# Half of the column transforms by mirror, a third bank for the MLP and a second for the first value products: a fused attention, Fourier-mix and MLP kernel on one core

## The chip, the cores and the metric

The kernel runs on one core of one Trainium2 chip. The metric is the device time of one launch in microseconds (us); less is better. The kernel before takes 309.21 us, the median of three runs from 308.92 to 309.44.

## The reference, cut to what matters

The batch has 4 items of 768 rows. Each item goes through attention in chunks (8 heads of 64, rows attend to a window of their neighbours and to 8 memory rows), then through a Fourier mix over rows and columns, then through a normalized MLP:

```python
x = attention(q, k, v, mem_k, mem_v)         # 4 x 768 x 512
X = np.fft.fft(np.fft.fft(x, axis=1), axis=2)
u = x + np.real(X)
un = (u - mean(u)) / sqrt(var(u) + 1e-6)     # over the last axis
out = u + np.maximum(un @ w_ch1, 0) @ w_ch2  # 512 -> 2048 -> 512
```

`x` is real, so the real part of its transform is the same at (row k, column j) and at (row -k, column -j), counted round.

## The kernel before, in words

**Order of the work.** Every piece of work is a task with an engine, an estimated cost, the tasks that it comes after, and buffers that it takes and gives back. `Plan.order` (L62) runs these tasks through a small clock of its own and writes down the order in which they start. That order is fixed when the program is built: on the chip each engine takes its instructions strictly in it and waits on semaphores. So an estimate that is wrong costs a wait, and nothing behind the waiting instruction can pass it on that engine. MLP matmuls are marked as fillers: they go wherever nothing else can start.

**Attention** (L692, per batch item four pairs of heads). q and k come by POOL's DMA queue (L286) and v by SP's (L289). TensorE turns q and k (L309), forms scores (L344), ScalarE takes the exponential (L355), TensorE forms the products with the values (`e_values`, L363), and VectorE divides by the sum and writes the rows to `xsb` (`e_norm`, L376). Each pair is done in two halves g. The value products of all halves go through one PSUM bank, tag `xa`. In the first batch item, which has no MLP work beside it, `Plan.order` fills idle time of TensorE with dummy matmuls (`e_fill`, L651, the rows named `idle`) until the first Fourier rows can start.

**Fourier mix.** VectorE folds the rows by symmetry and splits them into two half-precision parts. `g_rows` (first item, L517) or `e_rows` (L433) transforms along the sequence into PSUM tiles `ps`. ScalarE and VectorE bring them to `up` (`e_up` L448, `e_rest` L454), and a reversed copy goes to `dn` (`e_dn`, L459). `e_columns` (L537) transforms along the columns for six row tiles kt: eight matmuls of 256 columns for each, from `up` for kt 0 to 2 and from `dn` for kt 3 to 5, into PSUM tiles `pm`. `e_sum` (L549) adds them to `xsb` and frees the bank. `e_stats` (L553) and `e_un` (L560) give the centred rows. They are turned for the MLP by TensorE in the first item, and by SP's DMA transposes in the others (`e_flip`, L572).

**MLP.** In two halves sh of 384 rows: sixteen tiles `ph` of four matmuls each (`e_ch1`, L593), each emptied by ScalarE (`e_relu`, L600), then three tiles `pc` of sixteen matmuls (`e_ch2`, L606), each emptied by VectorE (`e_osb`, L613) and stored from ScalarE's queue (`e_out`, L619).

**PSUM.** Of eight banks, `tr` and `xa` have one each, `sc` two, and the tags `acc` and `mlp` two each. `ps` and `pm` use `acc`; `ph` and `pc` use `mlp`, but in the last batch item every third of their tiles uses `acc` (`mtag`, L588).

Of the kernel before, what the change touches and what calls it, by code (L numbers as in the profile page):

```python
# [31 lines left out]
def strided(src, off, dims):  # L32
    return bass.AP(tensor=src.tensor, offset=src.offset + off,
                   ap=[list(src.ap[0])] + [list(d) for d in dims])
# [105 lines left out]
def kernel(  # L140
# [49 lines left out]
    seq = [(b, pr) for b in range(B) for pr in (0, 2, 1, 3)]  # L190

    plan = Plan(dict(qs=NS, ks=NS, va=NV, kTb=NKT, qT=2, tr=1, sc=1, xa=1, e1=3,
                     xsb=3, fold=2, hl=1, up=4, dn=4, acc=2, mlp=2, un=6, unT=2, hT=1, osb=3))
    add = plan.add
    MLPS = 1000000

# [165 lines left out]

    def e_values(n, g):  # L363
        e1 = e1_of.pop((n, g))
        xa = aps.tile([P, 3, 2, 66], FP32, tag="xa", bufs=1, name="xa")
        xa_of[n, g] = xa
        for st in range(3):
            for hh in range(2):
                v1 = va[n % NV]
                for half in range(2):  # L370
                    t6 = 2 * st + half
                    nc.tensor.matmul(xa[64 * half:64 * half + 64, st, hh, 0:65],  # L372
                                     e1[:, hh, t6, :], v1[:, hh, 6 * g + t6, 0:65],
                                     start=True, stop=True)
# [11 lines left out]
            xa[:, :, :, 0:D], zs.unsqueeze(3).to_broadcast([P, 3, 2, D]), ALU.mult)  # L386


    zy_of, pq_of, ff_of, hl_of, ps_of, up_of, pm_of, un_of, tp_of = ({} for _ in range(9))
    mu_of, unT_of, rstd_of, g_of = {}, {}, {}, {}  # L390
    mid = cpool.tile([P, 2, NST, 1], FP16)
    mid32 = cpool.tile([P, NST, 1], FP32)
    warm = cpool.tile([P, 1], FP32)
    gate = cpool.tile([P, 1], FP32)

    def e_zy(b, par, c):
# [60 lines left out]
                                up[:, 0].rearrange("p k s -> p s k"), ALU.subtract)  # L457

    def e_dn(b, par, ab):  # L459
        dn = fpool.tile([P, 2, HS], FP16, tag="dn", bufs=4, name="dn")  # L460
        nc.vector.tensor_copy(dn, rev_ap(up_of[b, par, ab][2], HS, HS, [[2 * NK, 2]]))
        up_of[b, par, ab][1] = dn

    def g_zy(par, g):
        if g == 0:
# [82 lines left out]

    def e_sum(b, kt):  # L549
        uv = xs[b][:, kt, :].rearrange("p (j c) -> p c j", c=2)  # L550
        nc.vector.tensor_tensor(uv, pm_of.pop((b, kt)), uv, ALU.add)  # L551

    def e_stats(b, kt):  # L553
        if kt == 0:
# [17 lines left out]
    def e_flip(b, kt):  # L572
        if kt == 0:
            unT_of[b] = fpool.tile([P, NDT, S], FP16, tag="unT", bufs=2, name="unT")
        nc.sync.dma_start_transpose(unT_of[b][:, :, ts(kt, P)], un_of.pop((b, kt)))

    def e_unT(b, kt):
        if kt == 0:
# [6 lines left out]
        nc.gpsimd.tensor_tensor(rstd, rstd, mhalf, ALU.pow)  # L585


    def mtag(b, i):  # L588
        return "acc" if b == B - 1 and i % 3 == 2 else "mlp"

    ph_of, pc_of, hT_of, osb_of = ({} for _ in range(4))

# [18 lines left out]
                             start=(ht == 0), stop=(ht == NHT - 1))  # L611

    def e_osb(b, sh, stl):  # L613
        st = sh * 3 + stl
        osb_of[b, st] = osb = fpool.tile([P, DM], FP32, tag="osb", bufs=3, name="osb")
        nc.vector.scalar_tensor_tensor(osb, pc_of.pop((b, sh, stl)), rstd_of[b][:, st:st + 1],  # L616
                                       xs[b][:, st, :], ALU.mult, ALU.add)

    def e_out(b, st):  # L619
        nc.scalar.dma_start(out[b, ts(st, P), :], osb_of.pop((b, st)))  # L620


    t_zero = add("DVE", 0.2, e_zero, rank=-21)
    t_table = add("ACT", 1.4, lambda: nc.scalar.activation(warm, zero, AFT.Sin), [t_zero], rank=-3)
# [67 lines left out]
    def attention(n):  # L692
        nonlocal t_gate
        b, pr = seq[n]
        first = b == 0
        lq, lk = [add("POOL", 0.9, lambda i=i: e_load_qk(n, i), take=(("qs", "ks")[i],),
                      moved=1.3 if b else (2.1, 2.1, 1.4, 1.4)[n], late=0.0 if b == 0 else 2.0,
                      behind=t_gate if n == HP else t_ck.get(n - 1),
                      rank={0: -4 + i, 1: -1.2 + 0.1 * i}.get(n)) for i in range(2)]
        lv = add("SP", 2.5, lambda: e_load_v(n), [t_ones[n] if n < NV else None],  # L700
                 take=("va",), moved=4.0 if b else (4.4, 6.5, 4.9, 3.6)[n], late=0.0 if b == 0 else 2.0)
        t_lv[n] = lv
        t_ck[n] = lk
        if n == HP - 1:
            def e_gate():
                nc.gpsimd.tensor_copy(gate[64:65], va[n % NV][64:65, 1, NT - 1, 0:1])

            t_gate = add("POOL", 0.1, e_gate, [lv])
        tq = add("PE", 0.40, lambda: e_turn_q(n), [lq, t_idb], take=("tr",), give=("qs",))
        dve = ("DVE", nc.vector.tensor_copy) if n < HP else ("ACT", None)  # L710
        eq = add("ACT", 0.80, lambda: e_qT(n), [tq], take=("qT",), give=("tr",),
                 rank=SINES - 0.5 if n == 0 else None)
        ktag = "acc" if first else "tr"
        tk = add("PE", 0.43, lambda: e_turn_k(n), [lk, t_idb, t_kz if n == 0 else t_kzs], take=(ktag,), give=("ks",))
        mk = t_mk[n] = add("DVE", 0.2, lambda: e_mkT(n), [t_mkT, t_kTz[n % NKT], t_mk.get(n - 1)],
                           take=("kTb",))
        ek = add(dve[0], 1.25 if dve[1] else 1.04, lambda: e_kT(n, dve[1]), [tk, mk], give=(ktag,))
        for g in range(2):
            s_ = add("PE", 0.32, lambda g=g: e_scores(n, g), [eq, ek], take=("sc",),
                     give=("qT", "kTb") if g == 1 else ())  # L720
            t_sc[n, g] = s_
            x_ = add("ACT", 2.4 if (n, g) == (0, 0) else 1.12, lambda g=g: e_exp(n, g),
                     [s_, t_masks, t_after.get(n)], take=("e1",), give=("sc",))
            tag = "xa"
            v_ = add("PE", 0.85, lambda g=g: e_values(n, g), [x_, lv, t_low[n % NV]], take=(tag,),
                     rank=len(plan.tasks) + (50 if (n, g) == (2, 1) else 25) if first else None,
                     give=("e1", "va") if g == 1 else ("e1",))
            take = ("xsb",) if g == 0 and n % HP == 0 else ()
            t_norm[n, g] = add("DVE", 0.78, lambda g=g: e_norm(n, g),
                               [v_, t_norm[n - n % HP, 0] if (n % HP, g) != (0, 0) else None],  # L730
                               take=take,
                               give=(tag,))
        return x_
# [60 lines left out]
    def first_fourier():  # L794
# [37 lines left out]
                                              give=(tag,))  # L832
        return columns_of(0, t_rest)

    def fourier(b):
        nrm = [[t_norm[b * HP + i, g] for i in ii for g in range(2)] for ii in ((0, 1), (2, 3))]
        t_rest = {}
        zy = {}
# [24 lines left out]
        return columns_of(b, t_rest)  # L863

    def columns_of(b, t_rest):
        t_dn = {}
        for par in range(2):
            for ab in range(2):
                t_dn[par, ab] = add("DVE", 0.36, lambda par=par, ab=ab: e_dn(b, par, ab),
                                    [t_rest[par, ab]], take=("dn",))  # L870
        t_un = {}
        allr = list(t_rest.values())
        cols = {}

        def columns(kt):
            cols[kt] = add("PE", 0.9, lambda: e_columns(b, kt),
                           allr + [t_rows] + (list(t_dn.values()) if kt > 2 else []),
                           take=("acc",), rank=len(plan.tasks) + (15 if kt == 3 else 0),
                           give=("up",) * 4 if kt == 2 else ("dn",) * 4 if kt == 5 else ())

        sa = None
        columns(0)
        for kt in range(NST):
            if kt + 1 < NST:
                columns(kt + 1)
            su = add("DVE", 0.7, lambda kt=kt: e_sum(b, kt), [cols[kt]], give=("acc",))
            sa = add("DVE", 0.9, lambda kt=kt: e_stats(b, kt), [su, sa])
            un = add("ACT", 0.72, lambda kt=kt: e_un(b, kt), [sa], take=("un",))
            if b > 0:
                t_un[kt] = add("SP", 0.1, lambda kt=kt: e_flip(b, kt), [un, t_un.get(kt - 1)],  # L890
                               take=("unT",) if kt == 0 else (), give=("un",), moved=0.8,
                               loose=True)
                continue
            tp = add("PE", 0.26, lambda kt=kt: e_turn_u(b, kt), [un, t_idh], take=("mlp",),
# [8 lines left out]
    def mlp(b, t_un, rs):  # L903
        for sh in range(2):
            relu = []
            c2 = None
            for ht in range(NHT):
                ph = add("PE", 0.65, lambda sh=sh, ht=ht: e_ch1(b, sh, ht),
                         mlp_prev + [t_un[3 * sh + i] for i in range(3)] + t_w1,
                         take=(mtag(b, ht),), give=("unT",) if sh == 1 and ht == NHT - 1 else (),  # L910
                         rank=MLPS + len(plan.tasks), filler=True)
                relu.append(add("ACT", 0.5, lambda sh=sh, ht=ht: e_relu(b, sh, ht),
# [1 line left out]
                                take=("hT",) if ht == 0 else (), give=(mtag(b, ht),),  # L914
                                rank=RELU(len(plan.tasks))))
            for stl in range(3):
                st = 3 * sh + stl
                for part in range(4):
                    end = part == 3
                    c2 = add("PE", 0.88, lambda sh=sh, stl=stl, part=part: e_ch2(b, sh, stl, part),  # L920
# [2 lines left out]
                             rank=MLPS + len(plan.tasks), filler=True)  # L923
                os_ = add("DVE", 0.76, lambda sh=sh, stl=stl: e_osb(b, sh, stl), [c2, rs],
                          take=("osb",), 
                          give=(mtag(b, stl), "xsb") if st == NST - 1 else (mtag(b, stl),),
                          rank=RELU(len(plan.tasks)))
                mlp_prev[0] = c2
                add("ACT", 0.1, lambda st=st: e_out(b, st), [os_], give=("osb",), moved=0.9,
                    rank=RELU(len(plan.tasks)))  # L930

# [46 lines left out]
```

## Time and profile before

| what | us |
|---|---|
| median of three runs | 309.21 |
| the profiled execution: its time | 308.85 |
| the profiled execution: its span | 307.1 |
| busy: TensorE matmuls / VectorE / ScalarE / GpSimd | 289.5 / 171.2 / 161.5 / 40.8 |
| first value products start on the chain | 20.97 |
| first Fourier rows start on the chain | 42.57 |
| last matmul ends | about 303.1 |

The span is what the profiler saw from the first instruction to the last event. A matmul row's mean time is that of one instruction from entry to end; several are in flight at once, so that the pieces in the chain, which lists work back to back, give the price of one more matmul better than the mean does. A row "a <- b" in the list of waits says that a stood idle until b had ended.

### The profile page before, as it was taken

To read this page: it belongs to the slowest core of one execution; us is meant where nothing else is said; L and a number is where in the kernel's file an instruction comes from. 1 tells how busy PE (TensorE), PEld (TensorE's weight loads), DVE (VectorE), ACT (ScalarE), POOL (GpSimd) and SP (SyncE) were. 2 spreads that over 40 slices of the span, in tenths; PEclk is the share of its full clock that TensorE was granted. 3 is DMA by queue.
4 is the path that set the end of the run, shared out by engine and by line. 5 is a ranking of instruction groups with operands and counts; after the bars stand their busy time and mean duration, and the time that the engine had idled before them with its cause. 6 is when DMAs were issued, how large, how long until landed. Compare 5 with 4: busy or idle time off the path is not lost.

```text
span 307.1 us, 7496 instructions
## 1 busy us (share of the span) xinstructions
PE 289.5 (94%) x3148; PEld 181.5 (59%) x3148; DVE 171.2 (56%) x371; ACT 161.5 (53%) x291; POOL 40.8 (13%) x78
## 2 busy tenths in 40 slices
PE   1399999999999999999989999999999999999994
PEld 1267678866666676666756646675554554554541
DVE  7877895975397887797764399476101001001001
ACT  6656373689884666885257423743360450531710
POOL 8806421132201102000020000000200000000000
PEclk9999999999999999999999999999999999999999
DMA  6989999999944925821361011004201101001011
GB/s 114 197 171 167 204 205 196 198 204 178 193 72 91 203 45 111 136 47 40 89 137 36 2 46 59 0 19 102 86 2 40 64 2 68 34 2 71 31 36 68
DMA packets 60289, 28.93 MB, mean 94 GB/s; under 512 B 48480, under 2 KB 56672, under 8 KB 60256
## 3 DMA queue, kind: packets, MB, share of 16 engines
q1 hardware_dynamic: 47168, 11.61, 21.0%
q0 software_dynamic: 9344, 10.49, 20.8%
q10 hardware_dynamic: 3744, 6.36, 5.7%
q8 instruction: 25, 0.41, 0.5%
q14 instruction: 8, 0.07, 0.1%
HBM read 30.28 MB, written 6.29 MB: 119 GB/s over the span
## 4 chain that ended last, share of the span: by engine, by line
PE 91%; DMA 2%; POOL 2%; DVE 1%; ACT 1%; issue 1%; POOLq 0%; ACTq 0%
PE ph L596 28%; PE pc L610 27%; PE xa L372 9%; PE pm L545 7%; PE ps L440 5%; PE idle L654 5%; PE ps L534 4%; PE sc L351 3%; DMA qs<-in_q_dram 2%; PE trk L313 2%; PE trq L313 2%; DVE osb L616 1%; POOL qs L286 0%; ACT hT L603 0%; PE tp L570 0%
## 5 line engine op out<-in xcount | busy, mean ns | idle before, releaser
L603 ACT ACTIVATE hT<-ph 128x384 f16<-128x384 f32 x128 | 60.9, 492 | 63.0 <-PE ph L596 51.5
L596 PE MATMUL ph<-unT,w_sb 128*128 128x384 f16 x512 | 91.6, 326 | 2.2 <-ACT hT L603 1.1
L610 PE MATMUL pc<-w_sb,hT 128*128 128x512 f16 x384 | 86.9, 379 | 0.0
L596 PEld LDWEIGHTS <-w_sb 128*128 128x128 f16 x512 | 47.8, 97 | 36.8 <-issue 5.7
L616 DVE SCALAR_TENSOR_TENSOR osb<-pc,rstd,xsb 128x512 f32<-128x512 f32 x24 | 18.0, 749 | 82.5 <-PE pc L610 82.4
L610 PEld LDWEIGHTS <-hT 128*128 128x128 f16 x384 | 36.8, 98 | 41.2 <-issue 0.2
L359 ACT ACTIVATE e<-sc,mbias 128x384 f32<-128x384 f32 x64 | 33.8, 583 | 13.8 <-PE sc L351 11.3
L372 PEld LDWEIGHTS xa<-va,e 128*64 128x64 f32 x768 | 25.0, 137 | 7.8 <-issue 7.0
L372 PE MATMUL xa<-va,e 128*64 128x65 f32 x768 | 29.3, 226 | 0.0
L563 ACT ACTIVATE un<-xsb,mu_s 128x512 f16<-128x512 f32 x24 | 17.2, 720 | 14.9 <-DVE mu_s L558 14.8
L382 DVE RECIPROCAL zs<-xa 128x6 f32<-128x6 f32 x32 | 6.1, 191 | 25.6 <-PE xa L372 25.5
L452 ACT CAST up<-ps 128x386 f16<-128x386 f32 x16 | 9.7, 603 | 19.1 <-PE ps L440 13.5
L551 DVE TENSOR_TENSOR xsb<-pm,xsb 128x512 f32<-128x512 f32 x24 | 16.0, 675 | 4.4 <-PE pm L545 4.2
L383 DVE TENSOR_TENSOR xsb<-xa,zs 128x384 f32<-128x384 f32 x32 | 17.8, 557 | 1.1
L557 DVE BATCH_NORM_STATS2 st<-xsb 128x6 f32<-128x512 f32 x24 | 16.4, 684 | 0.5
L654 PE MATMUL idle<-dz 128*128 128x384 bf16 x71 | 15.3, 350 | 1.0 <-DVE zero L230 1.0
L322 ACT COPY qT<-trq 128x768 bf16<-128x768 bf16 x16 | 12.8, 798 | 5.6 <-PE trq L313 5.5
L286 POOL DMA_DIRECT2D ks<-in_k_dram x16 | 10.2, 635 | 35.0 <-PE trk L313 31.4
L584 POOL TENSOR_SCALAR rstd<-mu_s 128x6 f32<-128x6 f32 x4 | 1.0, 245 | 102.0 <-DVE osb L616 57.7
L313 PE MATMUL trq<-ident_b,qs 96*64 96x96 bf16 x256 | 9.4, 221 | 5.1 <-DMA qs<-in_q_dram 5.1
L286 POOL DMA_DIRECT2D qs<-in_q_dram x16 | 10.5, 659 | 25.2 <-PE trq L313 21.5
L456 DVE TENSOR_TENSOR up<-ps,up 128x386 f16<-128x386 f32 x16 | 9.6, 598 | 7.5 <-ACT up L452 7.5
(126 smaller groups left out, 343.5 us busy)
## 6 DMA issues: line engine op xcount, KB each, us to landing
va<-in_v_dram SPq DMA_DIRECT2D x32, 220.0 KB
out_dram<-osb ACTq DMA_DIRECT2D x24, 256.0 KB
w_sb<-in_moe_w_ch_dram POOLq DMA_DIRECT2D x8, 512.0 KB, 16.9
qs<-in_q_dram POOLq DMA_DIRECT2D x16, 192.0 KB, 5.7
ks<-in_k_dram POOLq DMA_DIRECT2D x16, 192.0 KB, 6.1
va<-in_mem_v_dram SPq DMA_DIRECT2D x32, 24.0 KB
va<-in_v_dram SPq DMA_DIRECT2D x32, 22.0 KB
va<-in_v_dram SPq DMA_DIRECT2D x16, 32.0 KB
```

Source lines behind the costliest of these rows:

```text
L286: nc.gpsimd.dma_start(dst[n % NS][0:QP], src[b, 2 * pr:2 * pr + 2].rearrange("h (p j) d -> p h (j d)", j=RB))
L313: nc.tensor.transpose(out_[64 * hh:64 * hh + 64, j * w:(j + 1) * w], src[:, hh, j * D:(j + 1) * D], eye)
L359: nc.scalar.activation(e1[:, :, :, ts(half, 32)], sc[:, :, 0:6, ts(half, 32)], AFT.Exp, bias=mbias[:, half:half + 1], scale=1.0 / math.sqr ...
L372: nc.tensor.matmul(xa[64 * half:64 * half + 64, st, hh, 0:65], e1[:, hh, t6, :], v1[:, hh, 6 * g + t6, 0:65], start=True, stop=True)
L383: nc.vector.tensor_tensor(xs[b][:, 3 * g:3 * g + 3, 2 * pr * D:(2 * pr + 2) * D] .rearrange("p s (h d) -> p s h d", h=2), xa[:, :, :, 0:D] ...
L545: nc.tensor.matmul(pm[:, par, :], lhs, rhs[:, par, :], start=(im == 0), stop=(im == 3))
L563: nc.scalar.activation(un, xs[b][:, kt, :], AFT.Identity, bias=mu_of[b][:, kt, 0:1], scale=-1.0)
L596: nc.tensor.matmul(ph[:, 0:384], w1_sb[:, dt, ts(ht, P)], unT_of[b][:, dt, sh * 384:(sh + 1) * 384], start=(dt == 0), stop=(dt == NDT - 1))
L603: nc.scalar.activation(hT_of[b, sh][:, ht, :], ph_of.pop((b, sh, ht))[:, 0:384], AFT.Relu, bias=0.0, scale=-1.0)
L610: nc.tensor.matmul(pc_of[b, sh, stl], hT_of[b, sh][:, ht, ts(stl, P)], w2_sb[:, ht, :], start=(ht == 0), stop=(ht == NHT - 1))
L616: nc.vector.scalar_tensor_tensor(osb, pc_of.pop((b, sh, stl)), rstd_of[b][:, st:st + 1], xs[b][:, st, :], ALU.mult, ALU.add)
L654: nc.tensor.matmul(fill_of[0][:, 0:384], dz, strided(dz, 0, [[0, 3], [1, P]]), start=True, stop=True)
```

## The change

Four things are changed together.

1. For the second to fourth batch items only three column tiles are transformed. The other three are the same numbers read backwards. `e_sum_back` adds them, reversed, to a mirrored copy of the rows `xr`. `e_back` writes the last three row tiles of `xsb` to DRAM in reversed order, and `e_mirror` reads them back, both on POOL's queue. `e_last_row` transforms the one row that has no partner, into row 0 of the first `pm` tile. The `dn` copies of these items are gone. A `pm` bank is no longer freed by `e_sum` but by `e_sum_back`.
2. These mirrored row tiles reach the output backwards: `e_out_rows` stores them to DRAM in the order in which they lie, and `e_out_back` copies them from DRAM to DRAM on SP's queue, reversed by rows and with the columns set right. The MLP takes the row tiles of these items in the order 0, 3, 4, 5, 1, 2.
3. Every third MLP tile uses an `acc` bank in all batch items, not in the last alone.
4. In the first batch item every second value product (g = 1) goes to a bank of `mlp` (tile `xo`), so that two banks take turns.

```diff
     def e_values(n, g):
         e1 = e1_of.pop((n, g))
-        xa = aps.tile([P, 3, 2, 66], FP32, tag="xa", bufs=1, name="xa")
+        if n < HP and g == 1:
+            xa = fps.tile([P, 3, 2, 66], FP32, tag="mlp", name="xo")
+        else:
+            xa = aps.tile([P, 3, 2, 66], FP32, tag="xa", bufs=1, name="xa")
...
+    def e_back(b):
+        r0 = xd[b % 2, 63:64]
+        nc.gpsimd.dma_start(bass.AP(tensor=r0.tensor, offset=r0.offset,
+                                    ap=[[64 * 3 * DM, 2], [-3 * DM, 64], [1, 3 * DM]]),
+                            xs[b][:, 3:6, :].rearrange("p t d -> p (t d)"))
+
+    def e_mirror(b):
+        xr_of[b] = xr = fpool.tile([P, 3, DM], FP32, tag="dn", bufs=1, name="xr")
+        xb = xd[b % 2]
+        nc.gpsimd.dma_start(xr[1:65], xb[64:128])
+        nc.gpsimd.dma_start(xr[65:128], xb[0:63])
+        nc.gpsimd.dma_start(xr[0:1, 0:2], xb[63:64, 1:3])
+        nc.gpsimd.dma_start(xr[0:1, 2:3], xb[63:64, 0:1])
+
+    def e_last_row(b):
+        pm = pm_of[b, 0]
+        for par in range(2):
+            todo = [(up_of[b, par, ab][0][:, part, HS:HS + 1], (cosD, nsinD)[ab])
+                    for ab in range(2 - par) for part in range(2)]
+            for i, (lhs, rhs) in enumerate(todo):
+                nc.tensor.matmul(pm[0:1, par, :], lhs, rhs[:, par, :], start=(i == 0),
+                                 stop=(i == len(todo) - 1))
+
+    def e_sum_back(b, kt):
+        pm, xr = pm_of.pop((b, kt)), xr_of[b]
+        y = xs[b][:, 3 + kt, :].rearrange("p (j c) -> p c j", c=2)
+        r = xr[:, 2 - kt, :].rearrange("p (j c) -> p c j", c=2)
+        nc.vector.tensor_tensor(y[:, :, 1:HD], strided(pm, HD - 1, [[HD - 1, 2], [-1, HD - 1]]),
+                                r[:, :, 1:HD], ALU.add)
+        nc.vector.tensor_tensor(y[:, :, 0], strided(pm, 0, [[2 * HD - 1, 2]]), r[:, :, 0],
+                                ALU.add)
...
     def mtag(b, i):
-        return "acc" if b == B - 1 and i % 3 == 2 else "mlp"
+        return "acc" if i % 3 == 2 else "mlp"
...
+    def e_out_rows(b, st):
+        nc.scalar.dma_start(od[b % 2, st - 3], osb_of.pop((b, st)))
+
+    def e_out_back(b, st):
+        t = st - 3
+        p0 = 1 if t == 0 else 0
+        src, r0 = od[b % 2, t, p0:P, :], S - P * t - p0
+        top = out[b, r0:r0 + 1, :] if r0 < S else out[b, 0:1, :]
+        half = [[1, HD]]
+        nc.sync.dma_start(bass.AP(tensor=top.tensor, offset=top.offset,
+                                  ap=[[HD, 2], [-DM, P - p0]] + half),
+                          bass.AP(tensor=src.tensor, offset=src.offset,
+                                  ap=[[HD, 2], [DM, P - p0]] + half))
+        if p0:
+            nc.sync.dma_start(out[b, HS:HS + 1, :], od[b % 2, 0, 0:1, :])
...
     def fourier(b):
+        t_x1 = add("POOL", 1.3, lambda: e_back(b), [t_norm[b * HP + i, 1] for i in range(HP)],
+                   moved=2.0)
+        t_xr[b] = add("POOL", 2.4, lambda: e_mirror(b), [t_x1], take=("dn",), moved=2.0)
...
+            kts = (0, 1, 3, 4, 2, 5)
...
+            else:
+                su = add("DVE", 0.8, lambda kt=kt: e_sum_back(b, kt - 3),
+                         [cols.get(kt), t_sum[kt - 3], t_xr[b]],
+                         give=("acc", "dn") if kt == 5 else ("acc",))
```

## The prediction

> **What bounds the kernel now.** I read the busy shares, the slices and the chain of waits first, then that chain piece by piece.
>
> ```profile
> PE 289.5 (94%) x3148; PEld 181.5 (59%) x3148; DVE 171.2 (56%) x371; ACT 161.5 (53%) x291; POOL 40.8 (13%) x78
> ...
> PE   1399999999999999999989999999999999999994
> ...
> DVE  7877895975397887797764399476101001001001
> ...
> PE 91%; DMA 2%; POOL 2%; DVE 1%; ACT 1%; issue 1%; POOLq 0%; ACTq 0%
> ```
>
> TensorE has work in every slice from 20 us on, and 91% of the chain lies on it. VectorE is busy until about 215 us and nearly empty behind it: the end is pure MLP, which the plan draws forward whenever TensorE would stand still. So matmuls taken out anywhere behind 65 us should come off the end one for one, as long as nothing new makes TensorE wait. Before 43 us it is different (pieces of the chain: start, us, what):
>
> ```profile
> 25.81 0.85 PE xa L372 x24
> 26.66 0.28 PE sc L351 x12
> 26.94 1.08 PE idle L654 x6
> 28.02 0.85 PE xa L372 x24
> ...
> 41.81 0.76 PE idle L654 x4
> 42.57 0.51 PE ps L534 x6
> ```
>
> Dummies are 49.3% of the chain from 20.5 to 43 us: TensorE follows a loop that runs through others here. Last, the end of a batch half:
>
> ```profile
> 217.98 0.02 issue
> 218.00 0.76 DVE osb L616
> 218.77 0.04 issue
> 218.81 10.53 PE ph L596 x60
> ```
>
> The chain names VectorE for 0.76, but the first `ph` tile runs beside it; what is lost must be taken from the stage's length.
>
> **The parts, against the profiled span of 307.1 us** (its time is 308.85, 1.75 more; the median 309.21 is 0.36 above that).
>
> *Columns removed.* Nine tiles of eight matmuls. The chain gives L545 7.1% of 307.1, so 21.8 us for 24 tiles: 0.91 each (single pieces are 0.87 to 0.98). 9 x 0.91 = 8.2 off, 7.8 to 8.8.
>
> *Last row added.* 3 x 6 matmuls of 256 columns with a one-column weight. Rows with such a weight cost what the full ones cost:
>
> ```profile
> L440 PE MATMUL ps<-cosS,lo 128*128 128x193 f16 x36 | 6.5, 245 | 0.0
> ...
> L440 PE MATMUL ps<-cosS,lo 128*1 128x193 f16 x18 | 3.3, 245 | 0.0
> ```
>
> So 18 x 0.114 (0.91 / 8) = 2.1 on.
>
> [...]
>
> *Start.* The loop of 2.05 to 2.2 us is: products 0.85, handoff, `e_norm` 0.19 + 0.56, handoff, then the bank is free. With two banks the next loop is scores 0.28, exponential 1.05 (27.05 to 28.10) and two handoffs of 0.11 (its scores end at 26.94), some 1.55. The built order of the changed kernel has 63 dummies for 71, with four between halves, so 0.85 + 0.28 + 4 x 0.178 (1.41 for eight) = 1.84 a half. Summing its pieces from 20.97 on, where the orders are still the same: 8 x 0.85, 6 x 0.28, two k turns 0.94, two q turns 0.80 and 51 dummies 9.1 make 19.3, against 21.6 now. The Fourier rows thus start at 40.3 for 42.57. One scores group and one q turn (0.74) only move behind them, so 8 x 0.178 = 1.4 is gained. VectorE must keep up: it is busy 18.2 of the 21.5 us from 21.0 to 42.5; 1.26 of it (two folds of 0.55, one small) moves behind the first `lo`, leaving 16.9 in 19.3. It fits barely. If not, nothing is gained: 0 to 2.3.
>
> *Third MLP bank.* Sixteen `ph` tiles at the end take 10.40 in the last item, which has three banks (261.51 to 271.91), and 217.98 to 229.34 = 11.36 where there are two. Two such halves of the third item: 1.9 off. Earlier, pieces of eight `ph` matmuls are 1.41 where 1.30 would be the last item's rate; I count nothing there, at most 0.11 x 32 = 3.5.
>
> *New waits.* A `pm` bank is now held from the columns to `e_sum_back`, and a third of the MLP stands in the same ring. VectorE needs, from the end of the first `pm` tile, two sums (0.68), two statistics (0.87) and one backward sum. I price the last by L551 (0.675) and, for its two-element part, the reciprocal of a PSUM tile (0.19): 0.87, together 4.0. Reading backwards costs nothing in this trace (L417 947 ns for 762 elements, L407 954 for 768). In the changed order, by these prices, TensorE reaches the third `pm` tile 5.4, 4.4 and 5.1 us after the first ended. Level on paper, with a few tenths to spare: a wait of 0 to 1 per item, and the same for MLP tiles behind `ps`. All waits of TensorE from 65 to 303 us sum to 2.3 now (idle in the windows). I take 1.5 on, 0 to 6: each side of the ring adds VectorE work of other kinds (0.75 osb or norm) when the plan's clock errs.
>
> *VectorE, ScalarE.* Twelve `dn` copies of 0.36 leave and nine small adds of 0.19 come: 2.6 less, hidden either way behind TensorE.
>
> *The mirror.* Per item POOL issues five DMAs (0.64 to 0.75 each) and waits in its queue for the first to land. Behind it stand q and k loads of the next item, which the order needs some 30 us later: hidden. The data, 768 KB each way, must be there when VectorE comes to the first backward sum. By the order that is some 25 us behind the last `e_norm`, in all three items. No row shows this transfer. The near ones:
>
> ```profile
> w_sb<-in_moe_w_ch_dram POOLq DMA_DIRECT2D x8, 512.0 KB, 16.9
> qs<-in_q_dram POOLq DMA_DIRECT2D x16, 192.0 KB, 5.7
> ```
>
> Below: 5.7 each. Above: 16.9 x 1.5 = 25 each, but that row is from a stretch where the DMA engines were full (share 1.02 to 1.21; 0.86, 0.41 and 0.10 later). Between, at the 205 GB/s of the fullest slice: 3.8 + (5.7 - 0.9) = 8.6 each, 17 the pair, hidden by 8. I take that, nearer to the q row as the queues have room. By the skill's page DMA: Bandwidth & Descriptors (Anatomy of one DMA) a fixed 2 us plus bytes at 436 GB/s would give, as an estimate, 3.8 each.
>
> *Output.* Stores through DRAM add a second trip for nine tiles. The last of them is emptied two `pc` tiles (2 x 3.47) before the end. Now the last store takes 3.2 from its osb's end (303.9) to the span's end; two in sequence take 6.4, and 6.9 + 3.2 are there. Hidden by 3.7; slower copies than 6.9 would show at the end.
>
> **Sum.** -8.2 + 2.1 - 1.4 - 1.9 + 1.5 = -7.9. Span 299.2, its time 300.9, median 309.21 - 7.9 = **301.3**.
>
> **Rivals.**
>
> *The start does not move.* VectorE sets it (slices of 8 and 9 there) and the dummies were harmless: 302.7. For: 18.2 of 21.5 busy. Against: it idles 1.6 and 1.9 at a time for value products.
>
> *The shared ring gives half back.* VectorE reaches the backward sums late by another osb, norm or fold, 1 to 2 us in each of three items and at some MLP tiles: 3 to 6 more waits of 0.75 to 1, 303 to 307. For: level on paper, VectorE 80% busy from 109 to 162. Against: MLP tiles in `mlp` stand between.
>
> *The mirror comes late: slower.* Its place is the first backward sum; it decides once the pair of transfers takes more than the 25 us. TensorE is in order, so its third `pm` and the `acc` MLP tiles stop. Beyond 25 + 8 in one item the whole gain is gone. At 25 each, the upper bound, and in the second item alone (the one with full queues): 50 - 25 = 25 late, 301.3 + 25 = 326. With 18 each in all three items: 11 x 3 = 33, 334. Against: the q row, and emptier queues from 85 us on.
>
> **How the numbers follow.** Forecast, 299 to 302.5: 0.53; the start unmoved: 0.10; the ring: 0.20; more gain than I count (the 3.5 of earlier `ph` pieces, no waits), 296 to 299: 0.04; the mirror, late enough to be slower: 0.11; a tie: 0.02. The low end is -7.9 - 1.5 - 0.6 - 0.9 (more at the start) = 298.3; the high end takes in the ring: 307. That holds 0.83. A change of over 0.2%, 0.6 us, is about what the measurement can tell: faster 0.87, same 0.02, slower 0.11.
>
> **What would show it.** Right: L545's column rows halve for three items, and 18 one-column rows of `pm` come; first `ps` at 40 to 41; `ph` halves of 10.4 in the last four; no wait of VectorE on `xr`. Wrong: TensorE waiting before `pm`, or before `ph` on VectorE's sums; `xr` landing more than 20 us behind its `e_norm`; a copy from DRAM to DRAM as the last event.

## The result, and the profile after

The changed kernel takes 337.53 us (median of four runs, 337.07 to 338.73) against 309.06 for the kernel before beside it (308.73 to 309.44): ratio 1.0927, 95% interval 1.0896 to 1.0958. The forecast was 301.3, in 298.3 to 307.0. It is wrong in sign.

First the same lines of the page as were shown of before: busy shares, slices of TensorE, its granted clock, and the chain.

```profile
PE 287.1 (85%) x3086; PEld 178.7 (53%) x3086; DVE 168.7 (50%) x368; ACT 162.9 (48%) x291; POOL 49.7 (15%) x93
...
PE   1499998999999699970079999999999999999940
...
PEclk9999999999999969995559999999999999999995
...
PE 77%; DMA 9%; SPq 5%; POOL 2%; DVE 2%; ACT 1%; issue 1%; POOLq 0%; DVEq 0%
```

TensorE and VectorE have less work than before; ScalarE has 1.4 us more and GpSimd 8.9, and neither is near full. TensorE's row has a hole of two slices (00) between two sevens, another at the very end (40, where it was 94), and a small one further left (the 6 between nines). TensorE has lost 14 points of the chain; DMA has 9% for 2%, and SyncE's queue (SPq), which was not listed before, 5%. So the time came in as waiting, in two large places and a small one, and transfers are behind all three.

Of the rows that the prediction named as signs of a right forecast, two came: the column rows halve for three items, with 18 one-column rows of `pm`, and the last `ph` halves take 10.4. Two did not: the first `ps` starts at 41.73, not 40 to 41, and VectorE waits 1.5 us for `xr`. Of the signs of a wrong one, two came as well: `xr` lands more than 20 us behind its `e_norm`, and a copy from DRAM to DRAM is the last event. The pieces of the chain (start us, us, what) in the start and in the last half, and the last sum of the kernel before:

```profile
22.12 0.88 PE xa L375 x24
...
24.18 0.85 PE xo L375 x24
...
41.73 10.89 PE ps L573 x120
```

```profile
303.38 10.40 PE ph L640 x64
313.78 10.37 PE pc L654 x48
324.18 0.75 DVE osb L660
```

```profile
303.15 0.75 DVE osb L616
```

The Fourier rows start 19.6 us behind the first value product instead of 21.6. But the last sum is at 324.18 where it was at 303.15, and the span ends 12.1 us behind that sum's end (337.0) where it had been 3.2. Hence two questions: 21.0 us ahead of the last sum, 8.9 behind it.

The wait list answers the first (who stood <- for what, us in total, times, longest):

```profile
POOL xr L480 <- DMA x_rows<-xsb: 55.1, 3, 19.5
...
PE ph L640 <- DMA unT<-un: 20.5, 1, 20.5
...
PE xa L375 <- DMA va<-in_mem_v_dram: 3.3, 1, 3.3
...
DVE xsb L498 <- DMA xr<-x_rows: 1.5, 1, 1.5
```

TensorE stands 20.5 us once, for `unT`: the transposed rows of item 1, which SyncE's DMA transposes bring. VectorE's wait for the mirrored rows `xr`, the place of the prediction's slower rival, is 1.5 us. The 3.3 us for `va` (values, by SyncE's queue) are the small hole; they come back below. How long the transfers took is in the DMA rows (count, size, median us from issue to landing):

```profile
x_rows<-xsb POOLq DMA_DIRECT2D x3, 768.0 KB, 19.8
xr<-x_rows POOLq DMA_DIRECT2D x3, 384.0 KB, 5.9
```

The write takes 19.8 us for 768 KB, the way back 5.9 to 6.6 for each of two parts. SyncE's queue, from 127 us on (start us, us, what it issues):

```profile
127.20 0.30 SPq L304 DMA_DIRECT2D va<-in_mem_v_dram  x1
139.83 1.63 SPq L295 DMA_DIRECT2D va<-in_v_dram  x2
141.50 0.96 SPq L304 DMA_DIRECT2D va<-in_mem_v_dram  x1
142.56 15.67 SPq L614 DMA_TRANSPOSE unT<-un  x3
158.33 0.62 SPq L299 DMA_DIRECT2D va<-in_v_dram  x1
...
165.76 1.21 SPq L614 DMA_TRANSPOSE unT<-un  x1
```

The `un` tiles of item 1 are all done by 131.3, so nothing but this queue holds the transposes. It stands from 127.5 to 139.8. Then three transposes take 15.67 us to issue; one of the three takes 11.8, where the median is 1.21. v loads follow, and only at 165.76 the fourth, which the first half of the MLP of item 1 needs: it lands at 170.3, and TensorE goes on. The write of the x rows was in flight from 138.8 to 158.6. The first gap is explained by SyncE's own waits (the third row here, with its longest of 12.3; the 18.7 lie earlier, from 80 to 99 us):

```profile
SPq L304 <- DMA out_dram<-osb: 18.7, 1, 18.7
...
SPq L614 <- DMA out_dram<-osb: 17.5, 1, 17.5
...
SPq L295 <- DMA out_dram<-osb: 13.5, 2, 12.3
```

SyncE, which stores no tile of item 0, waits for stores that ScalarE issues; the one behind the 12.3 leaves ScalarE at 137.63. Why a load of v should wait for a store of other data no view tells. The kernel before has four such waits, 42.6 us together and 13.2 the longest, with nobody behind them in need:

```profile
SPq L295 <- DMA out_dram<-osb: 31.0, 3, 13.2
SPq L304 <- DMA out_dram<-osb: 11.6, 1, 11.6
```

In the changed kernel the chain leads from such a store over SyncE's queue to the small hole too, TensorE's standstill from 115.1 to 118.4:

```profile
98.82 7.96 DMA out_dram<-osb
106.80 2.56 SPq L295
109.40 8.90 DMA va<-in_mem_v_dram
118.44 1.35 PE xa L375 x20
```

The first write of the x rows fills the time up to 106.9 there.

The table by windows (bounds, length, PE busy, PEld, DVE, ACT, POOL, clock, DMA share of 16 engines, GB/s) shows the stall and the end:

```profile
160.00:180.00 20.00, 9.65 (x109) 6.43 (x110) 1.87 (x4) 4.52 (x8) 0.70 (x2) 0.61 0.92 137
...
325.00:337.00 12.00, 0.00 (x0) 0.00 (x0) 0.00 (x0) 0.00 (x0) 0.00 (x0) 0.68 0.16 58
```

The granted clock is low behind both standstills: 0.50 from 118.0 to 124.5 us and from 170.3 to 175.5, and eight `ph` matmuls take 2.67 and 2.74 us there, where eight take 1.30 to 1.41 elsewhere. In the last 12 us no engine works, and the share of the 16 DMA engines is 0.16. What is left is ScalarE's last store, issued at 325.0, and the last copy from DRAM to DRAM, the second of this row of SyncE's queue, issued at 328.0:

```profile
320.08 8.51 SPq L675 DMA_DIRECT2D out_dram<-out_rows  x2
```

### The profile page after: what moved, and what is told of

It reads as the page before. It is cut to its first block, busy times and chain, and to the rows that moved or that the text cites. A ratio compares the mean times of both kernels' runs of the same rounds, so it can differ in the third digit from the quotient of the medians.

```text
span 337.0 us, 7397 instructions
## 1 busy us (share of the span) xinstructions
PE 287.1 (85%) x3086; PEld 178.7 (53%) x3086; DVE 168.7 (50%) x368; ACT 162.9 (48%) x291; POOL 49.7 (15%) x93
## 4 chain that ended last, share of the span: by engine, by line
PE 77%; DMA 9%; SPq 5%; POOL 2%; DVE 2%; ACT 1%; issue 1%; POOLq 0%; DVEq 0%
PE ph L640 25%; PE pc L654 24%; PE xa L375 6%; PE ps L445 4%; PE idle L713 4%; PE ps L573 3%; PE pm L584 3%; DMA va<-in_mem_v_dram 3%; SPq L295 2%; DMA out_dram<-osb 2%; SPq L614 2%; DMA qs<-in_q_dram 2%; PE sc L351 2%; PE trk L313 2%; PE trq L313 2%; DMA unT<-un 1%
## 5 line engine op out<-in xcount | busy, mean ns | idle before, releaser
L640 PE MATMUL ph<-unT,w_sb 128*128 128x384 f16 x512 | 91.5, 333 | 21.3 <-DMA unT<-un 20.5
L640 PEld LDWEIGHTS <-w_sb 128*128 128x128 f16 x512 | 48.9, 99 | 55.4 <-DMA unT<-un 21.0
L375 PE MATMUL xa<-va,e 128*64 128x65 f32 x672 | 26.5, 229 | 3.3 <-DMA va<-in_mem_v_dram 3.3
L375 PEld LDWEIGHTS xa<-va,e 128*64 128x64 f32 x672 | 22.5, 140 | 9.6 <-issue 4.4
L457 ACT CAST up<-ps 128x386 f16<-128x386 f32 x16 | 9.7, 604 | 15.2 <-PE ps L445 12.1
L286 POOL DMA_DIRECT2D ks<-in_k_dram x16 | 10.4, 649 | 40.0 <-PE trk L313 37.3
L386 DVE TENSOR_TENSOR xsb<-xa,zs 128x384 f32<-128x384 f32 x28 | 15.6, 558 | 1.0
L340 ACT COPY kTb<-trk 128x1056 bf16<-128x1056 bf16 x12 | 12.5, 1040 | 6.5 <-PE trk L313 6.4
L430 ACT CAST hi<-ff 128x768 f16<-128x768 f32 x12 | 9.9, 833 | 11.5 <-DVE ff L422 11.3
L713 PE MATMUL idle<-dz 128*128 128x384 bf16 x63 | 14.4, 365 | 1.0 <-DVE zero L230 1.0
L385 DVE RECIPROCAL zs<-xa 128x6 f32<-128x6 f32 x28 | 5.3, 188 | 17.9 <-PE xa L375 17.7
L590 DVE TENSOR_TENSOR xsb<-pm,xsb 128x512 f32<-128x512 f32 x15 | 10.1, 674 | 7.5 <-PE pm L584 7.3
## 6 DMA issues: line engine op xcount, KB each, us to landing
x_rows<-xsb POOLq DMA_DIRECT2D x3, 768.0 KB, 19.8
```

What stands on the lines that cost most here:

```text
L386: nc.vector.tensor_tensor(xs[b][:, 3 * g:3 * g + 3, 2 * pr * D:(2 * pr + 2) * D] .rearrange("p s (h d) -> p s h d", h=2), xa[:, :, :, 0:D] ...
L640: nc.tensor.matmul(ph[:, 0:384], w1_sb[:, dt, ts(ht, P)], unT_of[b][:, dt, sh * 384:(sh + 1) * 384], start=(dt == 0), stop=(dt == NDT - 1))
L713: nc.tensor.matmul(fill_of[0][:, 0:384], dz, strided(dz, 0, [[0, 3], [1, P]]), start=True, stop=True)
```

## The experiments

Four theories stood at the start; the letters are those of the expectations. *Two groups* (A): both new transfers have a dimension of 2 outermost (the write [2, 64, 1536], the output copies [2, 127 or 128, 256]) and run on few DMA engines. *Falling address* (B): they are slow because rows go to memory in reverse. *DRAM to DRAM* (D): such a copy is slow in itself. *SyncE's queue* (C): the transposes stand behind v loads that wait for ScalarE's stores, whatever the write costs. The kernel before takes 309.06 to 309.57 us (medians) beside these runs; all ratios are to it.

**e1 and e2: the write forward.**

```diff
-        r0 = xd[b % 2, 63:64]
-                                    ap=[[64 * 3 * DM, 2], [-3 * DM, 64], [1, 3 * DM]]),
+        r0 = xd[b % 2, 0:1]
+                                    ap=[[64 * 3 * DM, 2], [3 * DM, 64], [1, 3 * DM]]),
```

> The write of the rows to DRAM keeps its outer dimension of two halves, but goes forward instead of backward. The last three row tiles of items 2 to 4 then get the wrong rows added. Theory A (the write runs on two of sixteen DMA engines because its outermost dimension is 2): the write still lands after 18 to 21 us, the time stays at 335 to 340 us. Rival B (writing rows in falling address order is what is slow): the write lands within 8 us, and the time falls to 315 to 325 us.

And in e2 the whole tile in one, row by row:

```diff
+        nc.gpsimd.dma_start(xd[b % 2].rearrange("p t d -> p (t d)"),
+                            xs[b][:, 3:6, :].rearrange("p t d -> p (t d)"))
```

> The same forward write with 128 rows outermost; again the last three row tiles of items 2 to 4 get the wrong rows. Theory A: the write lands within 5 to 8 us, the first DMA transpose of the second item, which took 11.8 us to issue, takes 1.2 to 1.5, and the 20.5 us that TensorE waits for unT shrink to 6 or less; the time is 317 to 323 us, since the slow copies at the end stay. Rival C (the order on SP's queue, where transposes stand behind loads of v that wait for stores, makes that wait by itself): TensorE still waits 12 us or more for unT, 325 to 335 us. Rival B does not tell this run from theory A; the run before does.

Measured: 317.04 us (one run) and 318.9 (ratio 1.0295, 1.0255 to 1.0335); the write lands after 5.0 and 5.1 us. At first sight e1 speaks for the falling address: two groups, forward, and fast. It does not: two groups that follow each other in memory are one pattern of 128 rows, and the times say that it ran as that. Its issue takes 0.58 us as in e2, against 0.85 in the changed kernel. e1 is e2 once more and separates nothing. What e2 does show is that a fast write does not end the stall. TensorE still waits 7.3 us, over the 6 that *two groups* allowed and under the 12 of *SyncE's queue*:

```profile
PE ph L638 <- DMA unT<-un: 7.3, 1, 7.3
```

**e5: forward, in two groups that cannot be folded.** Each item's DRAM tile has two rows more, and the groups lie 65 rows apart.

```diff
+    xd = nc.dram_tensor("x_rows", [2, P + 2, 3, DM], FP32).ap()
...
+                                    ap=[[65 * 3 * DM, 2], [3 * DM, 64], [1, 3 * DM]]),
...
+        nc.gpsimd.dma_start(xr[1:65], xb[65:129])
```

> The x rows are written forward in two groups of 64 with one row left free between the groups, so that the two dimensions cannot be folded into one (in the run before they were: that was a write of 128 rows in one). Left out: the reversal, so the last three row tiles get wrong partners. Theory 'two groups': each write lands 19 to 21 us after its issue, as in the changed kernel, and the run takes 333 to 339 us. Rival 'falling address': it lands after about 5 us, as the forward write of 128 rows did, and the run takes 316 to 320 us.

Measured: 336.89 us (one run), and the DMA row

```profile
x_rows<-xsb POOLq DMA_DIRECT2D x3, 768.0 KB, 20.2
```

Forward and 20.2 us. So the falling address is not what makes 19.8; the two groups are.

The Trainium skill states the rule that the prediction lacked (DMA: Bandwidth & Descriptors, Why a DMA increments its semaphore by 16 and not by 1, and the same page's Rules for kernel authors): as a rule, the number of DMA engines is the largest one up to 16 that divides the size of the slowest dimension (the outermost above size 1) of both sides, so an outermost dimension of 2 keeps a transfer on two engines. The runs agree in order: two groups 19.8 and 20.2 us, eight groups 9.2 (e4), 128 rows 5.1 (e2). No view here counts the engines of a transfer.

**e3: the output copies in eight blocks of 64 columns.**

```diff
-        half = [[1, HD]]
-                                  ap=[[HD, 2], [-DM, P - p0]] + half),
+        half = [[1, 64]]
+                                  ap=[[64, 8], [-DM, P - p0]] + half),
```

> Only the copies from DRAM to DRAM are changed: eight blocks of 64 columns outermost instead of two of 256, so pieces of 256 bytes instead of 1 KB. Theory A: the copies land within 3 to 4 us, from the last osb to the end of the span there are 3 to 5 us instead of 12.1, the time is 329 to 331 us. Rival D (a copy from DRAM to DRAM is slow in itself, and smaller pieces make it slower): 12 us or more stay, 337 us or above.

Measured: 328.68 us (ratio 1.0616, 1.0568 to 1.0665), 8.85 less than the changed kernel and a little under the 329 to 331 expected. The last sum ends at 323.80 and the span at 327.1, 3.3 us behind it:

```profile
323.05 0.75 DVE osb L660
```

The copies still go from DRAM to DRAM with falling rows. The whole excess at the end goes with their two blocks; *DRAM to DRAM* falls. Part of it is the queue: here the last copy leaves SyncE at 318.95, ahead of the last sum, where it had left at 328.0, behind it.

**e4: eight groups in both trips.** The rows are reversed within groups of 16, and come back in eight parts (two more for row 0).

```diff
+                                    ap=[[16 * 3 * DM, 8], [-3 * DM, 16], [1, 3 * DM]]),
...
+        for g in range(8):
+            m = 15 if g == 0 else 16
+            nc.gpsimd.dma_start(xr[113 - 16 * g:113 - 16 * g + m], xb[16 * g:16 * g + m])
```

> The same result as the changed kernel: rows written in eight groups of sixteen, reversed within each group, and read back by eight loads that reverse the groups; the DRAM copies as in the run before. Theory A: both gains together, the write within 5 to 9 us, the end as short as before the change, 303 to 312 us. Rival C: the wait for unT stays at 12 us or more and the time is 317 to 327 us.

Measured: 317.42 us (ratio 1.0248, 1.0204 to 1.0293), outside what I expected of my own theory and inside the range of *SyncE's queue*. The write is down to 9.2 us, the end to 3.3, and TensorE still waits for `unT`:

```profile
PE ph L641 <- DMA unT<-un: 14.7, 1, 14.7
```

SyncE's queue in this run:

```profile
118.04 0.30 SPq L304 DMA_DIRECT2D va<-in_mem_v_dram  x1
132.58 0.80 SPq L295 DMA_DIRECT2D va<-in_v_dram  x2
133.42 0.31 SPq L304 DMA_DIRECT2D va<-in_mem_v_dram  x1
133.83 8.19 SPq L615 DMA_TRANSPOSE unT<-un  x3
...
149.20 3.79 SPq L615 DMA_TRANSPOSE unT<-un  x1
```

The three transposes now issue in 8.19 us for 15.67, but the gap ahead of them is there in full: 14.2 us. So there are two causes in a row. SyncE is held by a store of ScalarE until the second write of the x rows has just begun (131.7 here), and then the transposes issue beside that write. The first of them takes 11.8 us beside a write of 19.8 and 4.3 beside 9.2, but 1.3 beside 5.1 (e2) and 1.8 in e6 below, which has no write; three take 3.94 in e2 and 4.35 in e6. Beside a write of 5.1 us no slowing shows, beside the longer ones it does.

**e6 and e8: no trips at all**, with the stores of item 0 as they were (e6) and issued by GpSimd (e8). The sums read the x rows in place and every tile is stored at once.

```diff
-        r = xr[:, 2 - kt, :].rearrange("p (j c) -> p c j", c=2)
+        r = xs[b][:, 3 + kt, :].rearrange("p (j c) -> p c j", c=2)
...
-        nc.scalar.dma_start(od[b % 2, st - 3], osb_of.pop((b, st)))
+        e_out(b, st)
...
```

```diff
-        nc.scalar.dma_start(out[b, ts(st, P), :], osb_of.pop((b, st)))
+        (nc.gpsimd if b == 0 else nc.scalar).dma_start(out[b, ts(st, P), :], osb_of.pop((b, st)))
```

> No trip through memory: the backward sums read the x rows in place and every output tile is stored at once by ScalarE's queue (left out: both reversals; instructions of TensorE, VectorE and ScalarE as in the changed kernel). If the trips are all that the forecast mis-sized, the rest of its sum stands: 299 to 304 us, TensorE's wait for unT under 2 us. Rival 'SyncE's queue': the transposes of item 1 still stand behind v loads that wait for a store of ScalarE, TensorE waits 5 to 10 us for unT: 306 to 313 us.

> No trips (both reversals left out) and the stores of item 0 by GpSimd: both suspects gone. Both theories: 299 to 303 us, which is the forecast's sum without its trips; under that of e6 by what SyncE's waits cost without the trips (0 to 8 us).

Measured: e6 303.33 us (ratio 0.9801, 0.9762 to 0.984) and e8 299.15 (0.9662, 0.9634 to 0.969). Both times are as expected; TensorE's wait in e6 lies between the two theories (under 2, 5 to 10):

```profile
PE ph L640 <- DMA unT<-un: 2.8, 1, 2.8
```

Without the trips the forecast's sum stands: its 301.3 lies between the two runs, 2 us from each. SyncE's wait is still there in e6 (116.7 to 132.9, then three transposes in 4.35) and costs TensorE those 2.8 us; with the stores on GpSimd's queue it is gone, and so are 4.2 us.

**e7: eight groups in both trips, and the stores of item 0 by GpSimd.** The edits of e4 and the last of e8; nothing is left out.

> Eight groups in both trips, as the run of both in eight, and the stores of item 0 are issued by GpSimd instead of ScalarE, on a queue that SyncE does not share. Theory 'SyncE waits for ScalarE's stores': the 14 us waits of SyncE ahead of its first transposes go, TensorE's 14.7 us wait for unT with them: 303 to 308 us. Rival 'the wait is for something else in flight' (the x rows, v): the wait stays, 315 to 319 us. If GpSimd's own wait for the x rows delays the stores, osb runs out and VectorE's sums come late: above 318 us.

Measured: 299.63 us (ratio 0.9661, 0.9625 to 0.9697), under the 303 to 308 expected. This version beats both kernels. SyncE's queue:

```profile
114.42 0.80 SPq L295 DMA_DIRECT2D va<-in_v_dram  x2
115.27 0.31 SPq L304 DMA_DIRECT2D va<-in_mem_v_dram  x1
115.67 5.84 SPq L615 DMA_TRANSPOSE unT<-un  x3
...
128.67 1.22 SPq L615 DMA_TRANSPOSE unT<-un  x1
```

The first transposes leave at 115.67, 17 us ahead of the second write (132.75), and the fourth at 128.67, so none of the four that the first half needs meets it. The fifth, at 134.79, does and takes 2.98. No wait of TensorE for `unT` is left in the list. GpSimd now waits for the write in its queue (9.2 us the longest), with stores of item 0 behind it, and no wait of TensorE comes of that.

**e9: the changed kernel with only the stores moved.**

> The changed kernel with only one edit: the stores of item 0 are issued by GpSimd. The x rows stay in two groups (20 us a write) and the output copies in two blocks. Theory 'SyncE's queue makes the 20 us stall, the slow write only lengthens it': the first transposes leave some 18 us sooner, ahead of the second x write, TensorE's wait for unT goes; what stays is the end (12 us behind the last sum, 8.8 more than in eight blocks) and 0 to 6 us where a backward sum waits for the x rows: 308 to 316 us. Rival 'the slow write alone makes it': the wait for unT stays at 15 to 20 us and the run takes 325 to 335 us.

Measured: 313.08 us (ratio 1.0101, 1.0071 to 1.0131), as expected. The write is as slow as ever,

```profile
POOL xr L480 <- DMA x_rows<-xsb: 52.9, 3, 19.6
```

and yet TensorE does not wait for `unT`, nor VectorE for `xr`. That settles the stall: the slow write alone does not make it, and neither does SyncE's wait alone (2.8 us in e6 without a write, 7.3 in e2 beside a fast one). It takes both, one behind the other. The small standstill for `va` goes the same way: 3.3 us in the changed kernel, 3.8 and 3.9 in e3 and e5, which keep both, and none in e2, e4 and e9, which lack one. What e9 has over e7 is the end (from the last sum's start at 298.45 to 311.9 is 13.45, against 295.16 to 299.1, 3.94) and 3.3 us ahead of the last four halves, 2.0 of them one standstill of TensorE at 152.6 for which the list names no releaser; that I leave open.

**e10: before with the stores moved and nothing of the change.**

> The kernel before with the same edit of the stores and nothing of the change. SyncE's waits for ScalarE's stores (13.8 and 13.6 us there) go. If they were harmless, as its trace reads (TensorE did not wait for unT): 308.5 to 310 us, so that the gain of e7 belongs to the change. Rival: they cost something there too, as the 4 us between e6 and e8: 304 to 307 us.

Measured: 309.22 us, ratio 0.9996 (0.9976 to 1.0015). The waits of SyncE were harmless in the kernel before; the 3.4% of e7 belong to the change with its groups mended, not to the stores.

**e11 and e12: one part alone, put into before.**

```diff
-        return "acc" if b == B - 1 and i % 3 == 2 else "mlp"
+        return "acc" if i % 3 == 2 else "mlp"
```

> The kernel before with the third PSUM bank for the MLP tiles of items 0 to 2 and nothing else of the change. By the prediction's term: 1.9 us off, up to 5.4 if the earlier pieces gain too: 304 to 307.5 us. Rival 'the ring is shared': the ps and pm tiles wait for MLP sums, 309 to 312 us.

Measured: 310.13 us, ratio 1.0031 (1.0008 to 1.0054): missed, no gain but a small loss. That is in the rival's range, but its cause does not show: the list has no wait of TensorE before `ps` or `pm`. The four last `ph` stages are 10.40 there, as forecast. But the plan, with the third bank, brings TensorE to item 1's MLP while the transposes are in the queue:

```profile
112.59 25.10 SPq L295 DMA_DIRECT2D va<-in_v_dram  x2
137.74 0.45 SPq L304 DMA_DIRECT2D va<-in_mem_v_dram  x1
138.29 2.64 SPq L575 DMA_TRANSPOSE unT<-un  x2
```

Two v loads take 25.10 us of the queue, 24.5 of them a wait for ScalarE's store, and TensorE waits 3.7 for `unT`. The trace reads like e6's; a run of e11 with the stores moved was not made.

```diff
-        xa = aps.tile([P, 3, 2, 66], FP32, tag="xa", bufs=1, name="xa")
+        if n < HP and g == 1:
+            xa = fps.tile([P, 3, 2, 66], FP32, tag="mlp", name="xo")
+        else:
+            xa = aps.tile([P, 3, 2, 66], FP32, tag="xa", bufs=1, name="xa")
...
-            tag = "xa"
+            tag = "mlp" if first and g == 1 else "xa"
```

> The kernel before with the second bank for the value products of item 0 and nothing else of the change. By the prediction's term: 1.4 us off, 307.5 to 308.5 us, with the loop from the first value product to the first Fourier row in 19.3 us instead of 21.6. Rival 'VectorE sets the start': 309 to 310 us.

Measured: 307.06 us, ratio 0.9914 (0.9897 to 0.9931): 2.3 us off, more than the 1.4 forecast, at the far end of its 0 to 2.3 and under the 307.5 to 308.5 expected. In the chain the loop goes from

```profile
21.79 0.85 PE xa L375 x24
...
23.83 0.85 PE xo L375 x24
...
41.38 10.89 PE ps L537 x120
```

19.6 us, for 21.6 before. Alone this part gains 0.9%.

## Why the prediction was wrong, step by step

The stages of the three traces by the chain's pieces, in us, e7 being the change without its two faults:

| stage | before | after | e7 | forecast against before | e7 against before |
|---|---|---|---|---|---|
| start of the span to the first Fourier rows | 42.57 | 41.73 | 42.10 | -2.3 | -0.5 |
| from there to the last four MLP halves | 175.41 | 199.28 | 169.89 | -3.7 | -5.5 |
| the last four halves, to the last sum's start | 85.17 | 83.17 | 83.17 | -1.9 | -2.0 |
| last sum to the end of the span | 3.95 | 12.82 | 3.94 | 0 | 0 |
| span | 307.1 | 337.0 | 299.1 | -7.9 | -8.0 |

The 29.4 us that the changed kernel's second stage has over e7's are the two standstills, 20.5 and 3.3, and the low clock behind them: TensorE works 6.06 and 5.15 us at 0.50 there, which is, as an estimate, 5.6 lost. (The forecast's second stage is -8.2 + 2.1 + 1.5 and the 0.9 of its start that "only move behind".)

- **The mirror** is the step that failed, twice. "Between ... 8.6 each" priced the write by size from rows of other transfers, "nearer to the q row". It took 19.8, inside the bounds 5.7 to 25 but far from the value taken. The q row moves many partitions in one dimension; the new transfer has 2 outermost, and that was in the diff (e5: the two groups alone make it). The second failure is the place. I looked at who reads the data: VectorE, at the first backward sum. There the cover of some 25 us was right: 19.8 + 6.6 late by 1.5 once, and not at all in e9. I did not look at what else moves while the write lasts. "Behind it stand q and k loads ..., hidden" names GpSimd's queue; the queue that paid was SyncE's, whose transposes issued at 15.67 us for three instead of 3.9 to 4.4 (e2, e6).
- **SyncE's queue** does not stand in the prediction at all. Its four waits, up to 13.2 us, were in the trace of before, harmless (e10). The change brings TensorE sooner to item 1's MLP and makes the first half need the fourth transpose (row tiles 0, 3, 4). So a queue with slack became the bound. Alone it is 2.8 us of TensorE's waiting (e6), with the slow write 20.5, and 3.3 more for `va`.
- **Output**: "hidden by 3.7; slower copies than 6.9 would show at the end". They were slower, and showed: 12.1 behind the last sum's end for 3.2, gone with eight blocks (e3). The condition was written down and the price not worked out from the shape.
- **Slower rival**: its sign and 334 are near, but by another mechanism. It had the backward sums wait, 11 us in each of three items; what came is one wait of 20.5 before `ph`, in item 1, and the end. Being near is chance.
- **Start**: the loop was priced at 19.3 and is 19.6 to 19.8; "63 dummies" came. That the first Fourier rows are only 0.5 to 0.8 sooner is the loop's own start, 1.2 to 1.3 later (22.12 and 22.31 for 20.97). Of that, 0.4 and 0.6 are q's first load (7.37 and 7.56 us for 7.01). The other 0.8 are the last pieces ahead of the loop, which ran more slowly: five dummies 1.71 for 1.08, twelve score matmuls 0.43 for 0.28. They did so in e12 too, where the loop starts at 21.79. Why stays open.
- **Third MLP bank**: -1.9 forecast for the last halves, -2.0 measured in e7. In e11 the same gain is eaten by `unT`.
- **Columns, last row, new waits**: -3.7 forecast with the shared ring at +1.5, -5.5 measured in e7. The ring costs less than I took: TensorE's waits behind it in e7's list are 0.4 us for a sum (`xsb`) and 0.6 for ScalarE. The backward sum was priced at 0.87 and is 0.67 + 0.15 = 0.82.

So all of the sum's terms but two stand within 2 us, and their total is met within 0.1 by the span of e7. That it is so near is luck in part: the start gave 1.8 less than forecast and the second stage 1.8 more, and e7's median, 299.63, is 1.7 under the forecast. The two terms that cost "nothing, hidden", with SyncE's queue between them, made 37.9 us: 337.53 - 299.63. Moving the stores alone takes 24.5 of them away (e9), more blocks in the output alone 8.9 (e3). If the two add, which no run tested, 4.6 remain for the write's two groups; 3.3 is the difference of e9 to e7 ahead of the last four halves.

## What to carry to other kernels

Price a transfer by the shape of its access pattern first, the outermost dimension above all, and by its bytes second: here the same 768 KB took 5.0 to 20.2 us. A rearrangement that needs a short outer dimension is better cut into more groups. For a new transfer ask not only who reads it, but which queues issue while it is in flight, and who waits for those. A wait in a queue that costs nothing today is a term of the sum as soon as the change brings its reader forward: go through every engine's queue in the new order, those that only move data too.

## What the hardware showed that I had not expected

- One DMA of 768 KB takes 19.8 us in two groups, that is 40 GB/s, and no less where the DMA engines' share is 0.26 (207 to 226 us); it takes 9.2 in eight groups and 5.1 as 128 rows. How much of the difference between the last two is the reversal inside the groups stays open.
- A transpose that SyncE issues while such a write, from another queue, is in flight can hold that queue for 11.8 us instead of 1.2 (8.4 in e9). What holds it is not shown: the list puts 8.1 of the 11.8 down to ScalarE's copy to `kTb` and 7.9 of e9's 8.4 to another one (`hi`), and item 1's `un` tiles had long been ready (131.3 in the changed kernel).
- SyncE's loads of v wait for stores that another engine issues (18.7 us at most in the changed kernel, 24.5 in e11), and with the same stores from GpSimd, whose queue the profile lists as of another kind (software for hardware), that wait is gone (e6 against e8: 4.2 us).
- Behind standstills of 20.5 and 3.3 us TensorE's clock was 0.50 of full for some us, and the first pieces took twice as long. Behind the 2.8 us of e6 it was not (1.00 over the whole run), behind the 2.0 of e9 it was (0.81 over 150 to 158 us); what decides is open.
